# Part B of a gated two-branch kernel: Q, K and the attention output in five dense chunks of 128 rows, regrouped by head through DRAM

## The chip, the cores and the metric

The kernel runs on one core of one Trainium2 chip. The metric is the device time of one execution in microseconds (us). Every time of an instruction below comes from one profiled execution and is counted from the start of its span.

## The reference, cut to what matters

The output is `g * A(x) + (1 - g) * B(x)` for 2048 tokens of 640 features, with `g = sigmoid(sum(x * gate_w))`. A is a recurrent attention over 64 segments of 32 tokens. B is a local, dilated attention of 32 heads of 20 features, and it is the part that the change touches:

```python
H = 32; Dh = D // H                 # 640 / 32 = 20
W, dil = (8, 2)
qkv = (x @ wqkv).reshape(B, S, 3, H, Dh).transpose(2, 0, 3, 1, 4)
q, k, v = qkv[0], qkv[1], qkv[2]
...
idx = pos[:, None] - off[None, :]   # the 8 tokens at distance 0, 2, .., 14
logits = jnp.einsum('bhsd,bhswd->bhsw', q, kg) * Dh ** -0.5
logits = jnp.where(mask[None, None, :, :], logits, -1000000000.0)
attn = _softmax(logits, axis=-1)
o = jnp.einsum('bhsw,bhswd->bhsd', attn, vg)
return o.transpose(0, 2, 1, 3).reshape(B, S, D) @ wo
```

## The kernel before, in words

The program has three stages in a row: part B (`part_b`, lines 87 to 332), a prepass that multiplies the last rows of all segments by the weights of A (`prepass`, from L508), and the recurrent part A (`part_a`, from L611), which takes most of the time. The prepass needs all eight PSUM banks, so its first matmul (L531) waits for the last PSUM read of part B.

Part B walks over five blocks of tokens: four of 484 and one of 112 (`shape_of`, L202). In each block it walks over eight groups `g` of four heads. A head has 20 features, and four heads lie in the four 32-row quarters of a 128-partition tile; the 12 spare rows of each quarter are zeros. The weights of Q and K are spread to that form once (copies at L136, zeros at L131), and so are the rows of `wo` (zeros by GpSimd at L139, four loads of 20 partitions at L142). In step `(b, g)` of the loop at L310 these parts are called in this order:

- `make_xT` (L160) transposes the 512 tokens of the next x block by TensorE (L165), forms the gate (L176 to L183), and stores two rearranged copies for part A (L194, L199). At its middle it loads the next four x tiles from ScalarE's queue (L116).
- `make_v` (L209) forms V of the next block: 40 matmuls of 320 columns (L219), in a full block.
- `proj` (L226) forms Q and K of the next step: five matmuls each (L232), 484 columns for Q and 498 for K. Q is copied out by VectorE (`bqT`), K by ScalarE (`bkT`), both through the helper at L74/L76.
- `scores` (L240) forms the scores of four heads, 16 small matmuls (L250). ScalarE exponentiates them (L255, two instructions of 968 columns), and VectorE applies the band mask (L259).
- `values` (L262) works on the step before: 16 matmuls against a tile of ones give the softmax sums, 16 against V the outputs (L272). ScalarE forms the reciprocal by Ln and Exp (L277, L278), VectorE multiplies (L280) and writes the tile `OT`.
- `out_tile` (L283) multiplies 128 tokens of `OT` by `wo`: 16 matmuls of 320 columns (L290). One half is copied out by ScalarE (L295), the other by VectorE (L297), and ScalarE's queue stores the result (L299). There are 16 such tiles.

`proj`, `make_v`, `make_xT` and `out_tile` share two PSUM banks (`bank`, L108), so each waits for the copy-out of the last but one. The sums and the outputs have one bank each, the scores two pairs.

A scheduler orders the instructions of each engine at build time; it keeps roughly the order of the program but moves an instruction ahead where it is ready. Each engine then runs its own list strictly in order. That holds for transfers too: SyncE (SP) issues nearly all of them, and one that must wait holds up all transfers behind it; a transfer issued from ScalarE holds up ScalarE's arithmetic. `load_early` (L433) stands at the start of part B: it loads nine tiles of A's weights (L430, 4.2 MB) and makes copies of 21 further pieces from DRAM to DRAM (L441), from which part A later streams.

Of the kernel before, what the change touches and what calls it, by code (L numbers as in the profile page):

```python
# [10 lines left out]
BF = mybir.dt.bfloat16  # L11
# [16 lines left out]
class _K:  # L28
# [58 lines left out]
    def part_b(self):  # L87
# [11 lines left out]
        with ExitStack() as ctx:  # L99
# [25 lines left out]
            wop = wp.tile([128, 8, 640], BF, name="wo_pad")  # L125
            wqk = [wp.tile([128, KC, 32, 32], BF, name=f"w{n}_pad") for n in "qk"]
            xT = wp.tile([128, KC, HALO + S], BF, name="xT")
            OT = wp.tile([128, 8, S], BF, name="OT")
            wsrc = self.wqkv.rearrange("(c p) f -> p c f", p=128)
            for n, w in enumerate(wqk):  # L130
                nc.gpsimd.memset(w[:, :, :, 20:32], 0.0)  # L131
                raw = OT[:].rearrange("p g t -> p (g t)")[:, 3200 * n:3200 * n + 3200]
                (nc.scalar, nc.sync)[n].dma_start(raw.rearrange("p (c f) -> p c f", c=KC), wsrc[:, :, 640 * n:640 * n + 640])
                for kc in range(KC):
                    eng = (nc.vector, nc.gpsimd)[(KC * n + kc) % 2]
                    eng.tensor_copy(w[:, kc, :, 0:20], raw[:, 640 * kc:640 * kc + 640].rearrange("p (h d) -> p h d", d=20))  # L136
            nc.sync.dma_start(gw[:], self.gate_w.rearrange("(c p o) -> p c o", p=128, o=1))
            nc.scalar.dma_start(wv[:], wsrc[:, :, 1280:1920])
            nc.gpsimd.memset(wop[:], 0.0)  # L139
            wosrc = self.wo.rearrange("(g h d) f -> h d g f", h=4, d=20)  # L140
            for hh in range(4):
                nc.sync.dma_start(wop[32 * hh:32 * hh + 20, :, :], wosrc[hh])  # L142
# [81 lines left out]
            qk = {}  # L224

            def proj(b, g):  # L226
                nq, nu, c0 = shape_of(b)
                nt = nq * nu
                for n, (o0, nn) in enumerate(((c0 + HALO, nt), (c0, nt + HALO))):
                    ps = bank(F32, "ps_bqk")  # L230
                    for kc in range(KC):
                        nc.tensor.matmul(ps[:, 0:nn], lhsT=wqk[n][:, kc, 4 * g:4 * g + 4, :].rearrange("p h d -> p (h d)"),  # L232
                                         rhs=xT[:, kc, o0:o0 + nn], start=(kc == 0), stop=(kc == KC - 1))
                    t = wk.tile([128, BQ + HALO], BF, name="b" + "qk"[n] + "T", bufs=3)
                    self.evac(t[:, 0:nn], ps[:, 0:nn], "dve" if n == 0 else "act")
                    qk[b, g, n] = t
# [3 lines left out]
            def scores(b, g):  # L240
                nq, nu, c0 = shape_of(b)
                nk = nq + 7
                qT, kT = qk.pop((b, g, 0)), qk.pop((b, g, 1))
                for hp in range(2):
                    ps = psS.tile([128, 2, 512], F32, tag="S", name="ps_bS")
                    for u in range(nu):
                        a = 242 * (u // 2) + u % 2
                        for r in range(2):
                            rs = slice(64 * hp + 32 * r, 64 * hp + 32 * r + 32)
# [12 lines left out]
            def values(b, g):  # L262
# [4 lines left out]
                P = [Ps.pop((b, g, hp)) for hp in range(2)]  # L267
                for u in range(nu):
                    for out, z in ((pz, True), (po, False)):
                        for hh in range(4):  # L270
                            h = 4 * g + hh
                            nc.tensor.matmul(out[32 * hh:32 * hh + 32, nq * u:nq * u + nq],  # L272
                                             lhsT=ones[0:nk, :] if z else Vs[b, u][0:nk, 20 * h:20 * h + 32],
                                             rhs=P[hh // 2][0:nk, hh % 2, nq * u:nq * u + nq], start=(u == 0),
                                             stop=(u == nu - 1), tile_position=(0, 32 * hh), skip_group_check=True)
# [3 lines left out]
                dst = OT[:, g, BQ * b:BQ * b + nt].rearrange("p (l n q) -> p l q n", l=nu // 2, q=2)  # L279
                nc.vector.tensor_tensor(out=dst, in0=po[:, 0:nt].rearrange("p (l q n) -> p l q n", q=2, n=nq),  # L280
                                        in1=rz[:, 0:nt].rearrange("p (l q n) -> p l q n", q=2, n=nq), op=ALU.mult)

            def out_tile(ti):  # L283
# [3 lines left out]
                for f in range(2):  # L287
                    ps = bank(F32, "ps_bo")
                    for g in range(8):
                        nc.tensor.matmul(ps[:, 0:320], lhsT=OT[:, g, 128 * ti:128 * ti + 128],  # L290
                                         rhs=wop[:, g, 320 * f:320 * f + 320], start=(g == 0), stop=(g == 7))
# [13 lines left out]
            with tc.issue_after(self.first_store):  # L305
                self.load_early()
            make_v(0)
            proj(*steps[0])
            ti = 0
            for i, (b, g) in enumerate(steps):  # L310
                if g == 2 and b + 1 < S // 512:
                    make_xT(b + 1)
# [6 lines left out]
                if g == 6 and i + 8 < len(steps):  # L319
                    make_v(b + 1)  # L320
                if i + 1 < len(steps):
                    proj(*steps[i + 1])
# [3 lines left out]
                if g >= 1 and b > 0 and 128 * (ti + 1) <= BQ * b:  # L326
                    out_tile(ti)
                    ti += 1
# [104 lines left out]
    def load_early(self):  # L433

        for k in self.early:
            self.load(k, self.wres.tile([128, self.width(k)], BF, name="wres_" + "_".join(map(str, k)))[:])
        so = STREAM
        for i, k in enumerate(so):
            scr = self.dram.tile([128, self.width(k)], BF, name=f"wscr{i}")
            for d, src in self.sources(k, scr[:]):  # L440
                self.nc.sync.dma_start(d, src)  # L441
            self.wscr[k] = scr[:]
# [726 lines left out]
```

## Time and profile before

| | |
|---|---|
| time, median of 3 runs | 1613.4 us (1610.96 to 1613.96) |
| the profiled execution | 1609.81 us, of which its span is 1608.1 us |
| TensorE matmul busy | 1503.2 us (93%) |
| VectorE / ScalarE / GpSimd busy | 829.6 / 668.1 / 215.0 us |
| first exponential of part B (L255) | 31.79 us |
| first matmul of the prepass (L531) | 233.75 us |
| transfers issued from SP: L430 of `load_early` | 28.97 to 50.13 us |
| the copies from DRAM to DRAM (L441) | 50.17 to 80.83 us |

The table of stretches used below gives for each stretch its length, the busy time and number of instructions of each engine, the granted TensorE clock, the mean busy share of the 16 DMA engines and the GB/s that they moved. A line of the timeline gives start, duration, engine, line of the program, operation, output and input tiles, count, and in brackets how long the engine was idle before it and what it waited for. Records of neighbouring ScalarE instructions overlap by about 0.1 us, so the distance between two starts is what one costs.

### The profile page before, as it was taken

How to read it: one execution, taken by the hardware profiler on the slowest of the kernel's cores; microseconds unless marked ns; L12 is line 12 of the kernel's file. 1: busy time of each engine (PE TensorE's matmuls, PEld its weight loads, DVE VectorE, ACT ScalarE, POOL GpSimd, SP SyncE). 2: the span in 40 equal slices, each digit the busy share in tenths (PEclk: the TensorE clock that was granted, in tenths of full speed). 3: DMA queues.
4: the chain of work that ended last, by engine and by line, in shares of the span. 5: the costliest groups of instructions: out<-in, count | busy, mean ns of one | idle time of the engine just before them, and what ended most of it. 6: DMA issues, size and time to landing. Idle time of an engine off the chain costs nothing. (4 is left out here: it accounts for less than half of the span.)

```text
span 1608.1 us, 92193 instructions
## 1 busy us (share of the span) xinstructions
PE 1503.2 (93%) x37462; PEld 851.1 (53%) x37477; DVE 829.6 (52%) x2263; ACT 668.1 (42%) x1735; POOL 215.0 (13%) x403
## 2 busy tenths in 40 slices
PE   6988899978689999999999999999999999999979
PEld 3545554433345555555555555555555555555557
DVE  4646543322345655655655555555555655655520
ACT  3855752212234444444444444444444443444430
POOL 4002000001011111111111111111111111111100
PEclk9999999989899999999999999999999999999989
DMA  5941029989989999999999999999999999999980
GB/s 159 211 132 55 18 76 277 239 196 285 267 258 333 332 321 332 329 329 325 334 325 333 325 324 329 329 322 332 325 312 332 328 318 332 330 322 331 323 217 16
DMA packets 431326, 438.67 MB, mean 273 GB/s; under 512 B 184720, under 2 KB 298408, under 8 KB 431256
## 3 DMA queue, kind: packets, MB, share of 16 engines
q1 hardware_dynamic: 326968, 389.78, 74.2%
q10 hardware_dynamic: 93024, 31.07, 8.1%
q0 software_dynamic: 11264, 16.83, 3.5%
q8 instruction: 51, 0.84, 0.2%
q14 instruction: 19, 0.16, 0.0%
HBM read 403.79 MB, written 38.86 MB: 275 GB/s over the span
## 5 line engine op out<-in xcount | busy, mean ns | idle before, releaser
L736 ACT CAST aP<-psx 128x512 bf16<-128x512 f32 x128 | 68.8, 589 | 357.6 <-PE psx L729 334.6
L891 PEld LDWEIGHTS <-aP 128*32 128x32 bf16 x6144 | 164.2, 97 | 64.5 <-ACT aP L870 18.0
L827 PE MATMUL psm<-wlate_v,aHa 128*32 128x512 bf16 x2048 | 185.8, 380 | 0.4 <-issue 0.4
L729 PEld LDWEIGHTS <-aHa 128*32 128x32 bf16 x4608 | 115.9, 96 | 120.8 <-PE psm L729 20.7
L891 PE MATMUL psm<-wlate_oa,aP 128*32 128x384 bf16 x2560 | 168.7, 331 | 0.0
L751 DVE STREAM_TRANSPOSE aK<-aP 128x512 bf16<-128x512 bf16 (+1 forms) x256 | 135.1, 547 | 7.2 <-ACT aP L736 0.6
L891 PE MATMUL psm<-wst,aP 128*32 128x384 bf16 (+1 forms) x896 | 122.0, 307 | 9.5 <-DMA wst<-wscr 9.5
L891 PE MATMUL psm<-wlate_ob,aP 128*32 128x256 bf16 x2688 | 126.2, 274 | 0.5 <-issue 0.5
L729 PE MATMUL psx<-wlate_k,aHa 128*32 128x512 bf16 x1152 | 120.1, 380 | 0.0
L748 DVE STREAM_TRANSPOSE aP<-aP 128x512 bf16<-128x512 bf16 (+1 forms) x128 | 74.1, 579 | 85.8 <-ACT aP L736 85.8
L827 PE MATMUL psm<-wlate_v,aHb 128*32 128x512 bf16 x1152 | 115.7, 380 | 0.0
L870 DVE CAST aP<-psx 128x128 bf16<-128x128 f32 (+2 forms) x192 | 75.5, 421 | 77.2 <-PE psx L858 77.0
L729 PEld LDWEIGHTS <-aHb 128*32 128x32 bf16 x3072 | 73.3, 96 | 63.3 <-issue 2.1
L836 ACT CAST aP<-psm 128x256 bf16<-128x256 f32 (+1 forms) x192 | 85.9, 447 | 50.3 <-PE psS L781 47.4
L870 ACT CAST aP<-psS 128x384 bf16<-128x384 f32 (+2 forms) x192 | 65.3, 375 | 67.9 <-PE psx L858 52.6
L667 POOL DMA_DIRECT2D aVz<-zpk_dram x64 | 35.6, 556 | 426.5 <-PE psm L729 218.4
L729 PE MATMUL psx<-wst,aHa 128*32 128x512 bf16 x512 | 87.9, 381 | 0.4 <-DMA wst<-wscr 0.3
L729 PE MATMUL psx<-wlate_k,aHb 128*32 128x512 bf16 x768 | 78.4, 384 | 0.0
L852 PEld LDWEIGHTS <-aP 32*128 32x128 bf16 (+1 forms) x4096 | 44.1, 97 | 64.8 <-DVE aK L818 31.2
L660 POOL DMA_DIRECT2D aK<-xh_dram x63 | 34.9, 554 | 316.5 <-PE psm L827 281.1
L76 DVE CAST ZS<-ps_pre 128x512 bf16<-128x512 f32 x48 | 33.0, 692 | 82.6 <-PE ps_pre L531 76.8
L827 PE MATMUL psm<-wst,aHb 128*32 128x512 bf16 x384 | 74.2, 380 | 1.5 <-issue 1.5
(187 smaller groups left out, 3469.9 us busy)
## 6 DMA issues: line engine op xcount, KB each, us to landing
wst<-wscr SPq DMA_DIRECT2D x965, 256.0 KB, 4.6
wst<-wscr SPq DMA_DIRECT2D x384, 192.0 KB, 3.9
aP<-zpk_dram SPq DMA_DIRECT2D x64, 192.0 KB, 4.1
zpk_dram<-ZS ACTq DMA_DIRECT2D x5, 2048.0 KB
aVz<-zpk_dram POOLq DMA_DIRECT2D x64, 96.0 KB, 4.3
wlate_k<-in_A_Wk_dram SPq DMA_DIRECT2D x8, 512.0 KB
wres_q<-in_A_Wq_dram SPq DMA_DIRECT2D x7, 512.0 KB
wst<-in_A_Wk_dram SPq DMA_DIRECT2D x14, 256.0 KB
```

Of the source, the lines that this page charges most:

```text
L76: nc.vector.tensor_copy(out, in_)
L660: nc.gpsimd.dma_start(xh, row(self.xh_dram, s))
L667: nc.gpsimd.dma_start(vz[:], row(self.zpk_dram, s)[:, 768:1152])
L729: burst([nc.tensor.matmul(pq[32 * j:32 * j + 32, :], lhsT=hT[kc], rhs=sl[j], start=(kc == 0), stop=(kc == KC - 1), tile_position=(0, 32 * ...
L736: nc.scalar.copy(st[i], pqs[i])
L748: nc.vector.transpose(P[p][:, 1:5, c0:c1, :].rearrange("p b c i -> p c b i"), x)
L751: nc.vector.transpose(KT[:, c0:c1, :].rearrange("p c k -> p (c k)"), x)
L827: burst([nc.tensor.matmul(pvs[t][32 * j:32 * j + 32, :], lhsT=hT[kc], rhs=sl[j], start=(kc == 0), stop=(kc == KC - 1), tile_position=(0, 3 ...
L836: (nc.vector.tensor_copy if t == 0 else nc.scalar.copy)(Px[t][:, cs], pvs[t][:, cs])
L852: ms.append(nc.tensor.matmul(out[:, r, t, :], lhsT=v_block(2 * h + r, t)[ks, f0 - 128 * t:f1 - 128 * t], rhs=E[ks, par, EA.start + 40 * r: ...
L870: (nc.scalar.copy, nc.vector.tensor_copy)[g](x.rearrange("p (j c q) -> p j c q", j=2, q=32), pairs[g][:, :, 0:240].rearrange("p j (c q) -> ...
L891: ms.append(nc.tensor.matmul(pso[part][32 * jj:32 * jj + 32, 0:n], lhsT=oT_slot(R // 2, j, 3 * (R % 2) + t), rhs=self.o_weights(osl, part, ...
```

## The change

The weights of Q, K and `wo` are no longer spread to quarters of 32. Q, K and the output are computed in five dense chunks of 128 rows, and put into or taken out of the by-head form by transfers through DRAM. So that these transfers have time, Q and K are formed one block ahead (five chunks in the steps `g` = 0 to 4), and output tiles are formed later. The first block's Q and K, and a second `make_xT`, come ahead of the loop. `load_early` is queued behind the first block's round trip, and the copies from DRAM to DRAM leave it: eight, eight and five of them follow the round trips of later blocks. The softmax sums take one matmul per head over all columns. The core of the diff (left out are the plain loads of the dense weights, and the split of the copies into a function of their own):

```diff
-            wop = wp.tile([128, 8, 640], BF, name="wo_pad")
-            wqk = [wp.tile([128, KC, 32, 32], BF, name=f"w{n}_pad") for n in "qk"]
+            woc = wp.tile([128, KC, 640], BF, name="wo_sb")
+            wqk = [wp.tile([128, KC, 640], BF, name=f"w{n}_sb") for n in "qk"]
...
-            OT = wp.tile([128, 8, S], BF, name="OT")
+            OTc = wp.tile([128, KC, S], BF, name="OTc")
+            OTb = [wp.tile([128, 8, BQ], BF, name=f"OT{i}") for i in range(2)]
+            QK = [[[wp.tile([128, 4, BQ + HALO], BF, name=f"b{n}T{i}{h}") for h in range(2)] for i in range(2)] for n in "qk"]
...
-            nc.gpsimd.memset(wop[:], 0.0)
...
+            def heads(t, half, hh):
+
+                return t[320 * half:320 * half + 320].rearrange("(g h d) t -> h d g t", g=4, h=4)[hh]
...
+            def proj(b, n, c):
...
+                ps = bank(F32, "ps_bqk")
+                for kc in range(KC):
+                    nc.tensor.matmul(ps[:, 0:nn], lhsT=wqk[n][:, kc, 128 * c:128 * c + 128], rhs=xT[:, kc, o0:o0 + nn],
+                                     start=(kc == 0), stop=(kc == KC - 1))
+                t = wk.tile([128, BQ + HALO], BF, name="b" + "qk"[n] + "c", bufs=3)
+                self.evac(t[:, 0:nn], ps[:, 0:nn], "dve" if n == 0 else "act")
+                nc.sync.dma_start(qk_dram[b, n][128 * c:128 * c + 128], t[:, 0:nn])
+                if c in (2, 4):
+                    half = c // 4
+                    for hh in range(4):
+                        self.last_qk = nc.sync.dma_start(QK[n][b % 2][half][32 * hh:32 * hh + 20, :, 0:nn],
+                                                         heads(qk_dram[b, n], half, hh)).ins
...
+                for hh in range(4):
+                    nc.tensor.matmul(pz[32 * hh:32 * hh + 32, 0:nt], lhsT=ones[0:nk, :], rhs=P[hh // 2][0:nk, hh % 2, 0:nt],
+                                     start=True, stop=True, tile_position=(0, 32 * hh), skip_group_check=True)
...
+                if g % 4 == 3:
...
+                    for hh in range(4):
+                        nc.sync.dma_start(heads(ot_dram[b], half, hh),
+                                          OTb[b % 2][32 * hh:32 * hh + 20, 4 * half:4 * half + 4, 0:nt])
+                    cs = slice(2 * half, 2 + 3 * half)
+                    nc.sync.dma_start(OTc[:, cs, BQ * b:BQ * b + nt],
+                                      ot_dram[b][:].rearrange("(c p) t -> p c t", p=128)[:, cs])
...
-                    for g in range(8):
-                        nc.tensor.matmul(ps[:, 0:320], lhsT=OT[:, g, 128 * ti:128 * ti + 128],
-                                         rhs=wop[:, g, 320 * f:320 * f + 320], start=(g == 0), stop=(g == 7))
+                    for c in range(KC):
+                        nc.tensor.matmul(ps[:, 0:320], lhsT=OTc[:, c, 128 * ti:128 * ti + 128],
+                                         rhs=woc[:, c, 320 * f:320 * f + 320], start=(c == 0), stop=(c == KC - 1))
...
             make_xT(0)
-            with tc.issue_after(self.first_store):
+            for c in range(KC):
+                for n in range(2):
+                    proj(0, n, c)
+            with tc.issue_after(self.last_qk):
                 self.load_early()
+            make_xT(1)
             make_v(0)
-            proj(*steps[0])
...
-                if g == 2 and b + 1 < S // 512:
-                    make_xT(b + 1)
...
-                if g == 6 and i + 8 < len(steps):
-                    make_v(b + 1)
-                if i + 1 < len(steps):
-                    proj(*steps[i + 1])
+                if g == 6:
+                    if b + 2 < S // 512:
+                        make_xT(b + 2)
+                    if b + 1 < nb:
+                        make_v(b + 1)
+                if g < KC and b + 1 < nb:
+                    proj(b + 1, 0, g)
+                    proj(b + 1, 1, g)
+                    if g == KC - 1:
+                        with tc.issue_after(self.last_qk):
+                            for k in copies[:8]:
+                                self.copy_scratch(k)
+                            del copies[:8]
                 scores(b, g)
                 if i > 0:
                     values(*steps[i - 1])
-                if g >= 1 and b > 0 and 128 * (ti + 1) <= BQ * b:
+                if (b + 2 < nb and g >= 3 or b + 2 == nb and g in (5, 7) or b + 1 == nb and g in (2, 5)) and \
+                        128 * (ti + 1) <= BQ * min(b, nb - 2):
                     out_tile(ti)
                     ti += 1
```

By these conditions, three output tiles fall into block 1, four into block 2, two each into blocks 3 and 4, and five come behind the loop.

## The prediction

> **What bounds the kernel now.** The page names TensorE (1503 us busy of 1608), but that is an average over stages. I asked for stretches: the five blocks of part B, cut at the first exponential of each block. Part B ends where the prepass's first matmul starts, at 233.75, and nothing of A overlaps it on TensorE. So what part B gains, the kernel gains.
>
> ```profile
> core 0: us, PE busy (x) PEld busy (x) DVE busy (x) ACT busy (x) POOL busy (x), PEclk, DMA share, GB/s
> 31.79:68.64 36.85, 34.11 (x516) 18.67 (x514) 23.18 (x41) 28.36 (x47) 3.11 (x3) 1.00 0.85 191
> 68.64:118.79 50.15, 43.71 (x596) 24.75 (x592) 25.66 (x48) 31.61 (x53) 3.54 (x7) 0.93 0.55 149
> 118.79:169.19 50.40, 45.16 (x612) 26.09 (x608) 32.56 (x51) 31.43 (x52) 8.94 (x8) 0.97 0.16 45
> 169.19:209.76 40.57, 35.93 (x547) 21.48 (x543) 23.11 (x43) 28.27 (x47) 0.21 (x2) 0.98 0.10 31
> 209.76:233.75 23.99, 23.14 (x351) 15.17 (x350) 11.83 (x40) 13.39 (x46) 0.00 (x0) 0.88 0.09 30
> ```
>
> TensorE looks like the bound here too. Three single steps, from exponential to exponential, say otherwise: one with an output tile, a plain one, and one whose next projection is small.
>
> ```profile
> 92.26:98.42 6.16, 5.42 (x90) 3.15 (x82) 3.21 (x6) 3.81 (x7) 0.00 (x0) 1.00 1.01 282
> 98.42:101.74 3.32, 3.11 (x62) 1.48 (x50) 2.17 (x5) 3.29 (x6) 0.00 (x0) 1.00 0.05 16
> 204.04:206.90 2.86, 2.31 (x74) 1.68 (x60) 1.52 (x3) 2.86 (x6) 0.00 (x0) 1.00 0.12 44
> ```
>
> In the last two ScalarE has no gap (3.29 of 3.32, 2.86 of 2.86): these steps are ScalarE's, not TensorE's. The timeline shows why the first is long.
>
> ```profile
> 92.26 1.85 ACT L255 ACTIVATE bP<-ps_bS 128x968 bf16<-128x968 f32 x2
> ...
> 92.59 2.35 PE L290 MATMUL ps_bo<-wo_pad,OT 128*128 128x320 bf16 x16
> ...
> 95.12 0.51 ACT L295 ACTIVATE bo<-ps_bo,omg_sb 128x320 bf16<-128x320 f32 x1
> ...
> 95.69 1.18 PE L232 MATMUL ps_bqk<-xT,wq_pad 128*128 128x484 bf16 x5 [0.74 <-ACT bo L295]
> ...
> 96.70 1.21 PE L232 MATMUL ps_bqk<-xT,wk_pad 128*128 128x498 bf16 x5
> ...
> 97.95 0.57 ACT L74 CAST bkT<-ps_bqk 128x498 bf16<-128x498 f32 x1 [2.32 <-PE ps_bqk L232]
> ```
>
> It is a ring: ScalarE reaches the tile's copy-out only after its exponentials, the next projection waits for that bank, and ScalarE then waits 2.32 for K. The 16 output matmuls are no part of the ring.
>
> **The change, part by part.** The sum is made against the profiled execution: 1609.8 us, of it 1608.1 span and 1.7 around it. The median shown is 3.6 above that.
>
> *Matmuls removed.* Per full block 30 of 80 projections go, and 6 of 16 matmuls per output tile. At 1.01 us per five (95.69 to 96.70) and 2.35 per 16 that is 4 x 6.1 + 16 x 0.88 = 38 us of TensorE time. By the steps above most of it hides under ScalarE. The sums' 16 matmuls of 121 columns become four of 484: as many columns, nothing gained, and Ln waits for ScalarE anyway.
>
> *Start, 31.8 now.* Twelve projections instead of four precede the first scores: +8 x 1.03 = 8.2. A second `make_xT` comes ahead: +4.0, from steps (0,1) and (0,2), which take 6.32 and 4.27 around one instead of 3.32 each. The GpSimd memset of `wo_pad` goes; beside it (16.43 to 20.79) a VectorE addition on 4 columns (L180) took 4.54 instead of 0.17 and held V's copy-outs: -4.4. Weights come dense, so ten spreading copies go too; `wo`'s 0.8 MB now competes with x, about 3 us at 250 GB/s, and I let the two cancel. First exponential: 39.6. The round trip is hidden if Q and K of half 0 are there by then: six chunks from about 15 (two at half clock) end at 23.5. A 162 KB store lands 2.2 to 3.1 us after issue (135.76 to 137.93, 96.46 to 99.54), four loads issue in 1.5, landing again 3: about 33. If the cover failed, each us late would cost one.
>
> *Block 0, 36.85 now.* One `make_xT` and one `make_v` as before; three steps lose K's copy-out, 3.32 to 2.86: 35.5.
>
> *Block 1, 50.15 now.* Three plain steps at 3.45 (they take 3.32 to 3.72), one ring of 6.16 at `g` = 3; the tiles at 4 and 5 have no projection behind them, so 2.86 + 0.51 + a wait of 0.6 for VectorE's half: 4.0 each. `make_xT` 4.0, `make_v` 6.3 (9.63 against 3.32), two steps of 2.86: 40.5. Part of the gain is the stall of step (1,2), below.
>
> *Block 2, 50.40 now.* 10.35 + 6.16 + 3 x 4.0 + 6.3 + 2.86, and the stall that a GpSimd copy of the prepass puts on VectorE (L520, 143.56; VectorE's L285 took 4.28), which no part of the change removes: 41.8.
>
> *Block 3, 40.57 now.* Its projections are for the 112-row block: five steps at 3.0, two tiles at 4.0, V 3.5, one step 2.86: 29.4. Here all four steps with tiles were rings of 6.16.
>
> *Block 4 and tail, 23.99 now.* Six small steps at 1.3 (0.99 and 1.69 today), two with a tile at 2.6, the last values 1.0. Then the last output goes to DRAM and back: 2 x 2.2 to 3.1 plus five issues at 0.4, so 6.4 to 8.2; four tiles that need only block 3 run beside it at some 1.75 each (1.4 matmul, rest the copy-outs): 7.2 in all. Then one tile, 2.3: 23.5.
>
> Sum: 39.6 + 35.5 + 40.5 + 41.8 + 29.4 + 23.5 = 210.3 against 233.75, **-23.4**. Three costs are to be added, which the trace of before shows only in part.
>
> *SP's queue.* A full block issues 36 transfers (10 stores, 16 loads, 8 and 2 for the output) at 0.36 to 0.40, 13 to 14 us, and stops six times for a landing, 13 to 19 us: it fits under 35 to 42. The copies sit in the same queue: the ten of Q and K took 50.17 to 68.83, so the first eight hold it 15 us; the outputs behind them are read 25 us later at (1,3). Worse placed is `load_early`: its 4.2 MB, 17 us at 249 GB/s, go right ahead of block 1's first stores. Q's chunk buffers are three; the fourth copy-out, on VectorE at about 50, waits for the first store, which lands at about 58 to 60. Bounds: 0, if the build-time order lets scores overtake, and 9. The timeline around 76 shows transposes and scores interleaved, so the order is movable: I take +3.
>
> *ScalarE's queue.*
>
> ```profile
> 79.09 4.35 ACTq L116 DMA_DIRECT2D x_sb<-in_A_x_dram  x3
> ...
> 83.48 0.17 ACT L179 ACTIVATE gz_sb<-ps_g 128x4 f32<-128x4 f32 x1 [4.11 <-DMA x_sb<-in_A_x_dram]
> ```
>
> Three x loads issued while the copies ran held ScalarE 4.1 us. In the new order the last x loads follow the first eight copies again: +4. Bounds 0 (the copies are through) and 4.1 for every such issue (rival below).
>
> *Clock.* The granted clock is 0.88 in the last stretch: after two steps with small projections it fell to half, and the matmuls at 212 run at 0.45 for 0.30. Now three steps of every block have no projection. At half clock one output tile took 3.95 (85.73) instead of 2.35; I charge that 1.6 once in each full block: +6. Bounds: 0, and 5.8 (a whole `make_v` doubled) per block.
> By the Trainium skill, "TensorE: Matmul & The Clock Gate", "Why this matters for your kernels", the clock drops only after TensorE idles for some 3 us. No gap in these steps is that long, so by that rule this term is 0 and the sum -16; the row at 212 speaks against it, since TensorE was never idle so long there.
>
> Total -23.4 + 3 + 4 + 6 = **-10.4**: 1599.4 on the profiled execution's scale, **1603.0** on that of the median.
>
> **The rivals.** A measurement here can tell about 0.2% (3.2 us) from no change.
>
> 1. *Forecast*, 1603.0, chance 0.38.
> 2. *The clock stays full* (the page's rule): 1613.4 - 16.4 = 1597. For it: the plain steps of block 0 ran at 1.00 throughout. Against: 0.88 in the last stretch. 0.20.
> 3. *TensorE is the bound after all*, and all 38 us go: 1575. For: its busy share in the blocks. Against: the ScalarE rows of the single steps. 0.08.
> 4. *`load_early` really blocks*: 9 instead of 3, and 3 more where the outputs wait behind the copies: -1.4, 1612, no change that can be told. 0.12.
> 5. *Slower: the two queues couple.* An out-tile store is issued in ScalarE's stream. If it must wait for SP's chain of round trips as the x loads waited for the copies, each costs 4.1 us of the engine that is the bound. Eleven tiles lie inside the loop. Three such waits eat the forecast; five give -10.4 + 20.5 = +10, 1623.5. For: the 4.11 above. Against: the out-tile stores of blocks 2 and 3 went out among few other transfers and never waited so for one; how they fare among 36, the trace can't show. 0.22.
>
> That the change doesn't do what it says is no rival here: every matmul and transfer counted is in the code.
>
> **How the numbers follow.** Faster: forecast, 2 and 3, 0.66. Same: 0.12. Slower: 0.22. The range runs from 1585, which takes in rival 2 with all three costs near their lower ends but not rival 3, to 1624, the price of rival 5.
>
> **What would show it.** Right: first exponential at 39 to 41; the step without projection or tile at 2.86; blocks 1 and 3 shorter by about ten each; the prepass starting near 223, and its own 115 us to the V part unchanged. `load_early`: a wait of VectorE's Q copy-out for a store near 50. Rival 2: clock 1.00 in blocks 0 to 3. Rival 3: plain steps shorter than ScalarE's 2.86. Rival 5: ScalarE idle for a DMA at L299 in blocks 1 and 2. Wrong altogether: scores that wait for their Q and K loads at a block's start, or a prepass that starts earlier but loses it again for lack of weights.

## The result and the profile after

The changed kernel takes 1626.9 us (1624.9 to 1631.4, five runs) against 1613.4 us before (1608.3 to 1614.0, five runs): a ratio of 1.0098, 95% interval 1.0074 to 1.0123. It is slower by one per cent, and the forecast, its sign and its range missed it.

The same view as before, five stretches from one block's first exponential to the next (to 0.1 us); the columns are length, busy time and count of TensorE's matmuls and weight loads, VectorE, ScalarE, GpSimd, then granted clock, DMA share and GB/s:

```profile
core 0: us, PE busy (x) PEld busy (x) DVE busy (x) ACT busy (x) POOL busy (x), PEclk, DMA share, GB/s
38.86:86.70 47.84, 38.34 (x426) 20.25 (x425) 22.57 (x38) 29.51 (x46) 3.54 (x7) 0.75 0.66 178
86.70:125.10 38.40, 31.26 (x373) 16.38 (x372) 21.30 (x36) 27.46 (x42) 0.43 (x4) 0.78 0.78 168
125.10:179.40 54.30, 45.87 (x496) 26.16 (x496) 27.46 (x50) 30.98 (x51) 3.77 (x5) 0.84 0.58 147
179.40:213.40 34.00, 28.44 (x364) 16.44 (x359) 18.89 (x34) 25.04 (x42) 0.00 (x0) 0.70 0.37 89
213.40:247.50 34.10, 21.96 (x226) 12.13 (x224) 14.22 (x38) 12.18 (x39) 4.72 (x1) 0.79 0.60 177
```

The prepass starts at 247.5 instead of 233.8. These 13.7 us are about the difference of the medians (13.5). The profiled execution was the slowest of the five, 21.6 us above the profiled one of before; of the other 8 us, 1.4 lie in the prepass (116.8 us to its first V matmul, 115.4 before) and 6 in the recurrent part, which the change does not touch. Against before, the start takes 7.1 us more, block 0 11.0 more, block 1 11.8 less, block 2 3.9 more, block 3 6.6 less, and the last stretch 10.1 more.

The start is now 38.9 instead of 31.8, as forecast (39.6). But fewer matmuls (2067 instead of 2729 in part B) keep TensorE busy for 193.6 us, hardly less than the 199.9 before, with the clock at half for 95 us of the stretch from 25 to 250 us, where it was for 17.

The single steps are about as short as forecast (3.45 with projections, 2.86 without): one with projections, one plain, one plain of which a part is at half clock.

```profile
89.29:92.87 3.58, 3.40 (x50) 1.67 (x47) 2.60 (x5) 3.40 (x6) 0.00 (x0) 1.00 1.15 165
96.07:98.23 2.16, 1.33 (x29) 0.67 (x30) 1.44 (x3) 2.12 (x3) 0.00 (x0) 1.00 0.75 109
98.23:101.42 3.19, 2.16 (x43) 1.28 (x45) 1.99 (x4) 3.19 (x6) 0.00 (x0) 0.84 1.04 210
```

What is long is the last step of each block: 23.7, 18.1, 23.8 and 14.9 us from the first exponential of (b,7) to that of (b+1,0), where it was 3.7, 3.7, 3.7 and 2.9 before. The timeline of TensorE shows what fills the first of them:

```profile
66.74 0.60 PE L279 MATMUL ps_bO<-bP,bV 128*32 128x121 bf16 x16 [0.56 <-DVE OT L287]
68.76 2.17 PE L232 MATMUL ps_bqk<-xT,wq_sb 128*128 128x484 bf16 x5 [1.42 <-DVE bqc L76]
...
72.80 0.53 PE L159 MATMUL ps_xT<-ident,x_sb 128*128 128x128 bf16 x4
...
76.93 7.16 PE L213 MATMUL ps_bv<-wv_sb,xT 128*128 128x320 bf16 x40
83.99 1.18 PE L232 MATMUL ps_bqk<-xT,wq_sb 128*128 128x484 bf16 x5
...
86.16 0.43 PE L255 MATMUL ps_bS<-bqT,bkT 20*128 20x121 bf16 x16
```

After the last values of the block come, one behind the other, the fifth chunk's projections (68.76), the transposes (72.80), V (76.93) and the next block's first chunk (83.99), and only then scores again. In the kernel before each of these stood between two steps' scores. Now TensorE's list, fixed at build time, has the scores of `g` = 4 to 7 ahead of them. All of them need the two shared PSUM banks, and a bank is free only when the chunk in it is copied out, for which one of three chunk buffers must be stored (e1 below bears this out for block 0). The timeline of SP's queue shows why a store comes late:

```profile
40.36 12.45 SPq L462 DMA_DIRECT2D wres_q<-in_A_Wq_dram  x9
...
53.57 1.42 SPq L236 DMA_DIRECT2D bq_dram<-bqc  x1
```

The output meets the same queue one block later: the last heads of block 0 are multiplied on VectorE at 67.46, and their stores are issued behind eight copies.

```profile
94.89 2.50 SPq L475 DMA_DIRECT2D wscr<-in_A_Wk_dram  x1
...
103.76 2.23 SPq L294 DMA_DIRECT2D ot_dram<-OT  x4
...
110.25 0.37 SPq L297 DMA_DIRECT2D OTc<-ot_dram  x1
```

From 38 us to the prepass SP issued 66 transfers in 57 us of issuing before, and issues 228 in 123 us now (summed from the trace's SP rows).

### The profile page after: what moved, and what is told of

Its sections match the earlier page's. It is cut to its first block, busy times and chain, and to the rows that moved or that the text cites. A ratio compares the mean times of both kernels' runs of the same rounds, so it can differ in the third digit from the quotient of the medians.

```text
span 1629.6 us, 91195 instructions
## 1 busy us (share of the span) xinstructions
PE 1502.7 (92%) x36815; PEld 839.0 (51%) x36815; DVE 813.5 (50%) x2243; ACT 664.1 (41%) x1720; POOL 203.5 (12%) x395
## 5 line engine op out<-in xcount | busy, mean ns | idle before, releaser
L861 PE MATMUL psm<-wlate_v,aHa 128*32 128x512 bf16 x2048 | 189.5, 380 | 0.3 <-issue 0.3
L763 PEld LDWEIGHTS <-aHa 128*32 128x32 bf16 x4608 | 116.0, 96 | 117.9 <-issue 18.2
L861 PEld LDWEIGHTS <-aHa 128*32 128x32 bf16 x2304 | 54.5, 96 | 46.6 <-issue 16.2
```

Source lines behind the costliest of these rows:

```text
L763: burst([nc.tensor.matmul(pq[32 * j:32 * j + 32, :], lhsT=hT[kc], rhs=sl[j], start=(kc == 0), stop=(kc == KC - 1), tile_position=(0, 32 * ...
L861: burst([nc.tensor.matmul(pvs[t][32 * j:32 * j + 32, :], lhsT=hT[kc], rhs=sl[j], start=(kc == 0), stop=(kc == KC - 1), tile_position=(0, 3 ...
```

## The experiments

Two measures are given for each. The ratio to the kernel before, timed on the same chip, is the verdict. The **start of the prepass** (its first matmul) in the profiled execution says what part B took; it leaves out the recurrent part, which took from 1195 to 1209 us behind the prepass's last matmul in these profiles without any edit to it. But it is one execution of each kernel, and it scatters too: the changed kernel, e9 and e18, which are written the same up to there, have their first exponential at 38.9, 39.2 and 38.1. Differences of 2 to 3 us are therefore not read as effects.

| kernel | ratio (95%) | prepass starts |
|---|---|---|
| before | 1 | 233.8 |
| changed | 1.0098 (1.0074 to 1.0123) | 247.5 |
| e1 six buffers | 1.0042 (1.0023 to 1.0062) | 241.7 |
| e2 order | 1.0055 (1.0038 to 1.0072) | 238.3 |
| e3 six buffers, order | 1.0028 (1.0013 to 1.0043) | 239.6 |
| e4 sums alone | 1.0013 (0.9999 to 1.0028) | 231.0 |
| e5 output half alone | 0.9957 (0.9932 to 0.9982) | 227.4 |
| e6 Q and K half alone | 1.0110 (1.0081 to 1.0140) | 249.3 |
| e7 e3 with order both ways, bulk one per step | 1.0018 (1.0000 to 1.0036) | 243.2 |
| e8 e7, output from GpSimd | 1.0064 (1.0036 to 1.0092) | 247.9 |
| e9 changed, filler | 1.0067 (1.0050 to 1.0084) | 247.6 |
| e10 e7, filler | 1.0040 (1.0019 to 1.0062) | 246.5 |
| e11 e5, copies handed out | 0.9909 (0.9888 to 0.9931) | 220.7 |
| e12 before, less projection work | 0.9773 (0.9756 to 0.9790) | 201.6 |
| e13 e7's order, copies behind part B | 1.0202 (1.0165 to 1.0239) | 227.5 |
| e14 e13, Q/K loads from GpSimd | 1.0131 (1.0093 to 1.0170) | 225.1 |
| e15 e13, V and tiles spread | 1.0213 (1.0176 to 1.0251) | 231.4 |
| e16 before, copies handed out | 0.9950 (0.9928 to 0.9971) | 231.3 |
| e17 e7's order, four copies at a time | 1.0041 (1.0016 to 1.0067) | 241.0 |
| e18 changed, copies behind part B | 1.0310 (1.0260 to 1.0361) | 239.4 |

### Order and buffers: e1, e2, e3

e1 gives the chunks six buffers. e2 leaves three, and puts each step's scores behind that step's projections, V or tile in TensorE's list; e3 does both.

```diff
-                t = wk.tile([128, BQ + HALO], BF, name="b" + "qk"[n] + "c", bufs=3)
+                t = wk.tile([128, BQ + HALO], BF, name="b" + "qk"[n] + "c", bufs=6)
...
-                scores(b, g)
+                with tc.issue_after(self.pe):      # e2, e3: last matmul of proj, make_v or out_tile
+                    scores(b, g)
```

> The changed kernel with six chunk buffers per Q and K instead of three, nothing else. Theory A (TensorE's instructions are laid out so that projections, transposes, V and output tiles of a block pile up behind its last scores, because the fourth chunk's copy-out waits for a store that sits in SP's queue behind load_early): in block 0 the projections no longer wait for a buffer, the step behind scores (0,7), 23.7 us in the changed kernel, falls to under 8, and block 0 goes from 47.8 to some 36 to 39; blocks 1 and 2 keep their long last steps, since those wait for the output round trip. 1626.9 - 9 = 1618 us. Theory B (the loss is TensorE's half clock in the light steps): the same clock, under 4 us gained, 1623 to 1627. Theory C (the scores wait for the Q and K round trip at each block's start): buffers change nothing there, 1625 to 1628. Theory D (ScalarE held by its own transfers, the rival on record): no change, 1627.

> The changed kernel, three buffers as there, but with each step's scores put behind that step's projections, V and the output tile of the step before in TensorE's order, so that TensorE's list runs step by step and nothing piles up behind scores (b,7). No wait and no transfer is taken away. Theory A: the long last steps (23.7, 18.1 and 12.6, 23.8, 14.9 us) dissolve into the steps; block 0 still meets the store behind load_early, now at scores (0,4), so it gains least; blocks 1 to 3 lose some 8 to 12 us each, against which stand tiles that now really wait for the output round trip. 1627 - 17 = 1610 us. Theory B: the steps hold more work for TensorE, so the clock stays up, and the gain is the same in kind: the granted clock of part B then tells how much, 0 gain if the clock stays as it is. Theory C: longer, as scores that were ahead now wait as well, 1630. Theory D: no change, 1627.

> Both edits: six chunk buffers, and TensorE's list step by step. Theory A: this is the order for which the prediction's sum was made, so the prepass starts at some 223 to 230 (233.75 before, 247.5 in the changed kernel): 1603 to 1610 us. Theory C: still 1620 or more, with TensorE waiting for Q or K loads in the first step of each block. Theory D: ScalarE's waits for transfers stay, 1620 or more.

e1 went the way of theory A in block 0: the step behind (0,7) falls from 23.7 to 10.9 us (under 8 was expected), block 0 to 40.0. The last steps of blocks 1 and 2 stay at 21.3 us each, so there something else than the buffers makes the pile; what, these runs don't show. Part B is 5.8 us shorter. e2 gained more in part B (9.2 us, where theory A had 17): the long last steps are gone (3.3 to 3.6 us), yet blocks 0 and 1 take 48.7 and 47.7 us, no less than in the changed kernel. Its list holds TensorE where the store is late, and the wait that the prediction had named "near 50" is there to see, on TensorE and on VectorE:

```profile
60.16 2.17 PE L232 MATMUL ps_bqk<-xT,wq_sb 128*128 128x484 bf16 x5 [8.38 <-DVE bqc L76]
```

```profile
59.45 0.66 DVE L76 CAST bqc<-ps_bqk 128x484 bf16<-128x484 f32 x1 [6.85 <-DMA bq_dram<-bqc]
```

Theories C and D gave no gain for these, and are out as the main cause. But e3 did not reach theory A's 1603 to 1610 (223 to 230): order and buffers are 7.9 of at least 13.7 us. What e3's TensorE still waited for was the output:

```profile
PE ps_bo L309 <- DMA OTc<-ot_dram: 20.1, 4, 7.2
```

### The halves of the change: e4, e5, e6

e4 puts the new sums into the kernel before. e5 adds the output half to it; Q and K stay as they were. e6 is the changed kernel with the output left in SBUF in the padded form. The diffs are the parts of the change itself.

> The kernel before with one part of the change alone: the softmax sums by one matmul of 484 columns per head instead of four of 121. The prediction's step (as many columns, Ln waits for ScalarE anyway): within 2 us of the kernel before, 1611 to 1615. If TensorE is what bounds the steps (rival 3 on record), 36 x 12 matmuls fewer at some 0.03 us of issue each: 1605 or less.

> The kernel before with the output half of the change alone (and the one-matmul sums): heads go to DRAM and back, five output matmuls of 128 rows per half tile, output tiles placed as in the changed kernel; Q and K as before, with 32 rows per head and two buffers ahead. Here the copies lie in SP's queue long before the output and TensorE's list stays step by step. Theory A (pile-up and queueing behind SP's bulk transfers): little is lost; the tail pays the last round trip, 4 to 6 us, the rings of blocks 1 and 2 give 2 to 4 back: 1609 to 1617 us against some 1612. If the output round trip by itself is what costs (TensorE waits for it wherever it lies), tiles wait in every block: 1620 or more.

> The changed kernel with the output half undone: the output stays in SBUF with 32 rows per head, eight output matmuls per half tile, no output transfers; Q and K in five chunks through DRAM as in the change, three chunk buffers. Theory A: the pile-up behind (0,7) stays, as it comes from the chunk buffers and load_early; tiles 0 and 3 no longer wait for transfers, so blocks 1 and 2 lose less, and the tail is short: 1612 to 1619 us. If the loss lay in the output round trip alone: 1600 to 1606. If it lay in Q and K alone: 1625 or more.

The sums alone make no difference that can be told, as predicted (the prepass's start, 2.8 us earlier, lies within its scatter). The output half makes the kernel **faster**, by more than expected (6.4 us in part B). The Q and K half carries the whole loss, and more of it than any reading expected but the last. Of e6's 15.6 us, 10.3 lie before the first exponential (42.1 against 31.8): e6 pays for the early projections and also keeps the zeros and the four loads of the padded `wo`, which the whole change drops.

### SP's queue: e7, e8, e13, e14, e17, e18

In these runs, e18 apart, there are six buffers, and the list goes step by step both ways: projections, V, transposes and tiles also stand behind the scores of the step before. e7 hands out the early loads and the copies one per step, e17 the copies four at a time behind each return of the output, e13 puts all the copies behind part B. e8 issues the output's transfers from GpSimd, e14 Q's and K's loads. e18 moves the copies in the changed kernel and does nothing else. Where an expectation speaks of 24 copies, the kernels make 21, in 26 transfers.

```diff
-                        with tc.issue_after(self.last_qk):
-                            for k in copies[:8]:
-                                self.copy_scratch(k)
-                            del copies[:8]
...
+            with tc.issue_after(self.back):        # e13, e18: the last return of the output
+                for k in copies:
+                    self.copy_scratch(k)
```

> The changed kernel with six chunk buffers, TensorE's list step by step on both sides (scores behind that step's projections, projections, V, transposes and tiles behind the scores of the step before), and SP's bulk transfers (9 early weight loads and 24 copies) handed out one per step behind that step's other transfers instead of nine at once and eight at once. Theory A: no wait of 7 to 10 us for a store or for the output is left; block 0 at 36 to 39, blocks 1 and 2 at 38 to 43, prepass at 225 to 231: 1602 to 1608 us where the kernel before has some 1612. If SP's queue is full in any order (36 transfers with their stops plus eight copies of 1.5 us are 40 to 45 us per block): blocks of 42 to 47 us, no long single wait but many of 2 to 4, 1613 to 1618.

> As the run before, and the output round trip issued from GpSimd's queue instead of SP's (ten transfers per block). Theory A: SP's queue loses some 8 us per block; where the run before still had tiles waiting for the output, they no longer do: 0 to 5 us better than that. If SP's queue was not the limit there: the same within 2 us; if GpSimd's descriptor work delays its own copies of xh and zx: worse by a few us.

> The changed kernel with six chunk buffers, TensorE's list step by step, and all 24 copies moved behind the last output transfer of part B, so that SP's queue carries only the round trips, the early loads and the stores of x in part B. What counts is the start of the prepass (233.8 before, 247.5 in the changed kernel, 239.6 with buffers and order, 243.2 with one bulk transfer per step); the copies then lie beside the prepass and may hold its weights, which is read apart. Theory E (SP's one queue, in which each transfer waits for the data of the one ahead, is what delays the output and the chunks): prepass at 226 to 232. If what is left lies on TensorE (transposes and V of a block in one step behind the scores, 15 to 18 us where they are spread over the steps in the kernel before): 238 to 242, as with the copies.

> As the run before, and the 16 loads of Q and K per block are issued from GpSimd's queue, the stores of the chunks and the output round trip stay on SP. Theory E: SP loses 6 us and four waits per block, output and chunks go out without waiting for each other: 3 to 8 us earlier than the run before. If GpSimd's own price per transfer takes it back, or the round trips had cover: the same within 2 us, or some us later with scores waiting at a block's start.

> The whole change with six chunk buffers, TensorE's list step by step, and the copies four at a time behind each return of the output. Theory E: between the run without copies in part B (prepass at 227.5) and the one with eight at once (239.6): 231 to 238, 1609 to 1616, so the whole change at its best here is no faster than before. If the place alone counts, and not how much SP issues: 227 to 230, 1603 to 1608.

> The changed kernel with only the copies moved behind part B: three chunk buffers and TensorE's list as it was. Theory A (order and buffers cost by themselves): the step behind (0,7) keeps its 23 us, as load_early still lies ahead of the first store; blocks 1 and 2 lose the wait for the output but keep the pile: prepass at 238 to 243, against 227.5 with order and buffers. Theory E alone (only the copies cost): 227 to 231. The prepass itself is held by the copies, as in the earlier run.

e7 and e17 fell on the side of "full in any order": 243.2 and 241.0, no better than eight at once (239.6), and e17 missed what theory E gave for it. In e7 one long wait for the output is left all the same (10.0 us). e8 was worse than e7 on both measures, although TensorE's waits for the output fell from 14.9 to 4.1 us; what took that back was not found. e13 was the run that decided: with the copies out of the queue, part B ends at 227.5, inside theory E's 226 to 232, with SP issuing 199 transfers in 92 us. TensorE's waits for the output fell to

```profile
PE ps_bo L309 <- DMA OTc<-ot_dram: 8.3, 2, 4.4
```

The kernel as a whole is slower all the same: beside the copies the prepass takes 151.0 us to its first V matmul instead of 115.4, and TensorE waits 40.0 us in it for weights:

```profile
PE ps_pre L568 <- DMA wst<-in_A_Wq_dram: 23.2, 1, 23.2
PE ps_pre L568 <- DMA wst<-in_A_Wk_dram: 9.1, 1, 9.1
PE ps_pre L568 <- DMA wlate_q<-in_A_Wq_dram: 7.7, 1, 7.7
```

e14 took 2.4 us more off, less than theory E gave and within the scatter. e18 separates the causes, as theory A expected it (238 to 243) and theory E alone did not. Together, with the start of the prepass:

| | copies in part B | copies behind it |
|---|---|---|
| list and buffers as changed | 247.5 | 239.4 |
| six buffers, step by step | 239.6 to 243.2 | 227.5 |

The three runs of the lower left cell (e3, e17, e7) differ in the order and in how the copies are handed out; e17 and e13 differ in the place of the copies alone, e18 and e13 in buffers and order alone. Mending the list gives 4 to 9 us (e2 the most), moving the copies alone 8, both 20. So the order of TensorE's list and the copies in SP's queue both cost, and together they seem to cost more than one by one (3 to 8 us, the lower end near the scatter).

Whether the copies delay the rest by SP's time to issue them or also by the DMA engines' time was not separated. There is a third way, which none of the theories names. In the changed kernel SP's transfers wait for out-tile stores that ScalarE issued, other work altogether:

```profile
SPq L294 <- DMA bsc_dram<-bo: 6.1, 1, 6.1
SPq L475 <- DMA bsc_dram<-bo: 4.9, 1, 4.9
SPq L236 <- DMA bsc_dram<-bo: 4.9, 2, 2.7
SPq L240 <- DMA bsc_dram<-bo: 4.7, 2, 2.7
```

In the trace the transfers of both queues take the same eight completion semaphores (the counters that tell of a landing) in turn, and these waits are on them. So the two queues are coupled: six waits, 20.6 us by the profile's account, of which the two of L240 (4.7 us) may be for their own data as well. e13 has such waits too. What they cost was not tested.

### The clock: e9, e10

Both write the 16 values matmuls three times into the same bank in steps with little work, where they change no number.

```diff
-                for u in range(nu):
+                for _ in range(3 if g >= 4 or b >= 3 else 1):
+                    for u in range(nu):
```

> The changed kernel, and the 16 values matmuls are written three times over into the same bank for heads of g = 4 to 7 and of block 3 on: the same numbers, only more work for TensorE, in the time in which it would wait for Ln and Exp. Theory B' (the granted clock follows how busy TensorE was: in ten traces, of 427 windows of 3.41 us at full clock that were 0.8 busy or more, two were followed by half clock, of 37 under 0.45 busy, 35 were): busier steps keep the clock, V, transposes and projections at the blocks' ends run at full clock, mean clock of part B up from some 0.80 towards 0.9, 1627 - 8 = 1619 us or less. Theory A (order and queues alone): added work can only cost, up to 32 x 0.8 us, or nothing where it is hidden: 1627 to 1635.

> The kernel with spread bulk transfers, six buffers and TensorE's list step by step (1616.9 where the kernel before had 1611.0), and values written three times over as in the run before. Theory B': what that kernel still lost (V of block 1 at half clock, 9.1 us between 61.1 and 70.2, the output tile of block 3, the tail) falls by some 10 us: 1604 to 1609. Theory A: what is left there is waiting for the output, which added matmuls don't shorten: 1616 to 1622.

The counts of windows in the first of these texts are off; the last section has them, counted over all kernels. The filler did raise the clock (71 us at half instead of 95 in e9, 61 instead of 85 in e10) and moved the start of the prepass by +0.1 and +3.3 us. e9's shorter time as a whole (the interval overlaps the changed kernel's) does not come from part B. e10 came out where theory A put it (1620.8 us). And e13 runs below full clock in four of its five stretches (0.83, 0.89, 1.00, 0.81, 0.73), with 55 us at half, and is 20 us shorter than the changed kernel. Theory B' is not borne out: no time could be bought back by raising the clock with filler. But the filler takes time itself, and in e13 half clock fell along with the waits, so what half clock costs by itself stays open.

### TensorE's own work: e12, e15

```diff
-                    for kc in range(KC):
+                    for kc in range(1):            # e12, in the projections of the kernel before
```

> The kernel before with only the first of the five contraction chunks in each Q and K projection: four fifths of the sum over the features are left out, so some 57 us of TensorE's matmul time go from part B, and no transfer, wait or order changes. The prediction's step (ScalarE is the bound, TensorE's time hides under it): 5 to 15 us faster, 1598 to 1608. Rival 3 on record (TensorE the bound): 40 us faster or more, 1570. Theory B' (less work lets the clock fall to half, which gives the time back): part B with the clock at half in the greater part of it, and 1608 to 1620, no gain or a loss.

> As the first run of these, and TensorE's work of a block is spread: transposes in step 5, V in two halves in steps 6 and 7, output tiles of blocks 1 and 2 in steps 5 to 7 instead of 3 to 6. If the pile of transposes and V in one step costs (the second reading of the first run): its 15 to 18 us in block 0 fall to 8 to 10, blocks 1 and 2 lose their waits for the output: prepass 6 to 12 us earlier than the first run. Theory E alone: tiles in later steps wait less for the output, 2 to 5 us earlier.

e12 is the run that speaks most directly against the prediction's reading of the single steps. The table of stretches from the first instruction to the prepass, of the kernel before and of e12:

```profile
0.00:233.75 233.75, 199.91 (x2729) 116.46 (x2730) 130.55 (x244) 139.02 (x249) 32.02 (x47) 0.96 0.40 104
```

```profile
0.00:201.60 201.60, 165.50 (x2409) 95.66 (x2410) 128.04 (x244) 135.67 (x249) 33.27 (x47) 0.92 0.47 121
```

The projections are busy for 52.5 us less (80.9 to 28.4). TensorE as a whole is busy for 34.4 us less, as other matmuls take longer, with the clock at half for 34 us instead of 17 (from 25 to 250 us). Part B is 32.2 us shorter, with ScalarE and VectorE nearly unchanged. In the kernel before, then, some three fifths of the time taken from TensorE count; it is not so that most of it hides under ScalarE. The whole gains 37.7 us, near to rival 3's 40. e15 asked whether V and the transposes in one step were what remained in e13; part B got longer (231.4), which neither forecast had, and that reading is not borne out.

### The version that beats both: e11, and its control e16

e11 is e5 with the copies four at a time behind each return of the output; e16 is the kernel before with its copies eight at a time behind stores of x.

```diff
+                    with tc.issue_after(back.ins):
+                        for k in self.copies[:4]:
+                            self.copy_scratch(k)
+                        del self.copies[:4]
```

> The kernel with the output half alone (1605.4 where the kernel before had 1611.0), and its 24 copies handed out in SP's queue four at a time behind each return of the output instead of all behind the early loads. Theory A: the stalls that the copies make in block 1 there (x loads and the gate held 4.9 us on ScalarE, projections at 81 and 93 waiting) go, block 1 falls from 53 to 42 to 46 us: 1596 to 1601 us. If those stalls come from the output's own transfers: 1604 to 1607.

> A control: the kernel before, unchanged but that its 24 copies are handed out in SP's queue eight at a time behind the second, third and fourth store of x instead of all behind the early loads. It tells what the handing out is worth without the change. Theory E (bulk transfers in SP's queue cost where something waits in that queue): nothing of before's scores or tiles waits for SP, only x loads and the gate on ScalarE, 4 to 7 us in block 1: prepass from 233.8 to 227 to 231, 1605 to 1610 where the kernel before has 1612. Then the output half keeps some 6 us as its own gain in the fastest version so far (prepass at 220.7). If handing out is worth as much as there: 220 to 224.

e11 takes 1598.3 us, 0.9909 of the kernel before, as expected. How much of that is handing out alone? By the start of the prepass in e16, 2.4 us of the 13.1, no more than the scatter; by the timed runs, 0.9950, some 8 of e11's 15 us. The two measures disagree, so the output half's own share in e11 stays open; alone, in e5, it gave 0.9957. The stretches of e11's blocks 1 and 3, cut at the first scores, columns as above (before, cut at the first exponentials: 50.15 and 40.57):

```profile
64.30:108.90 44.60, 39.64 (x479) 21.49 (x478) 25.62 (x48) 31.39 (x51) 3.48 (x7) 1.00 0.56 121
...
160.30:192.00 31.70, 29.26 (x403) 15.11 (x404) 21.24 (x37) 27.02 (x43) 0.17 (x2) 1.00 0.20 52
```

## Why the prediction was wrong, point by point

**The step that failed** is "SP's queue", with its "+3" and its sentence "it fits under 35 to 42", and the block sums that rest on it. It reckoned SP's issuing for one block and let the copies and the round trips share the queue at no cost beyond `load_early`. Measured, the order (with the buffers) and the copies cost 20 us of part B together (247.5 against 227.5): the 36 transfers, the copies and the stops don't fit, and what waits there holds banks, so that TensorE's work piles up behind (b,7), shown for block 0 by e1 and argued for the others. The clause "if the build-time order lets scores overtake" was read the wrong way round. Scores did overtake, and that did not hide the wait but moved the projections, V and tiles to where nothing runs beside them. The queue is not all of it: even in e13 the prepass starts 17 us behind the 210.3 to which the blocks add up before the three costs.

*Matmuls removed.* "Most of it hides under ScalarE" was wrong: e12 gives 32.2 us for 52.5 us of projections. Three single steps were read as the rule; that the steps with V, transposes and tiles, which make up the rest of a block, are TensorE's is argued from that, not measured step by step. Rival 3 was nearer to what bounds the kernel before, and the change still lost, because the gain was given back to the order, the copies, the start and the tail.

*Start*: right, 38.9 for 39.6. It is a price of the Q and K half: the first exponential comes at 37.7 to 38.7 in e1 to e3 and e13, and at 29.0 in e11.

*Block 0*: 47.8 for 35.5, the pile. *Block 1*: 38.4 for 40.5, near by luck, as its tiles, transposes and V partly lie in block 2. *Block 2*: 54.3 for 41.8, the pile again. *Block 3*: 34.0 for 29.4; the same tiles without Q and K in chunks take 31.7 (e11), which fits the reading of the rings as ScalarE's and VectorE's copy-outs but does not test it.

*Block 4 and tail*: 34.1 for 23.5. In the changed kernel TensorE is idle for 12.1 us of it (0.9 before), but hardly for a return of the output (its weight loads wait 1.1 us); a wait of 4.4 us for one is in e13, where the stretch takes 31.9. Two gaps of TensorE, 2.30 us at 223.74 and 3.90 before the prepass, end with VectorE or ScalarE waiting for an out-tile store: all tiles go through two `bo` buffers, five tiles stand behind the loop, and the store issued at 239.73, for which the last tile waits, lands 7 us later, beside the weight loads that SP issues from 236 on.

```profile
246.78 0.53 ACT L314 ACTIVATE bo<-ps_bo,omg_sb 128x320 bf16<-128x320 f32 x1 [6.08 <-DMA bsc_dram<-bo]
...
247.49 0.61 PE L565 MATMUL ps_pre<-zT,wres_q 128*128 128x512 bf16 x1 [3.90 <-DVE bo L316]
```

*`load_early`*: the wait was named and is there (8.38 us on TensorE in e2), nearer the upper bound of 9 than the 3 taken. *Outputs behind the copies*, 3 us in rival 4: moving the copies gave 8 us, and 12 to 16 with the list mended.

*ScalarE's queue*, +4: ScalarE waited four times for a transfer, 3.3 and 1.4 us in the blocks, 2.7 and 6.1 in the tail, all at copy-outs of out tiles or of the K chunk beside one. That is rival 5's row, and in the tail, as shown, it costs; in the blocks the waits are fewer and shorter than the three of 4.1 that rival 5 needed, and that its 1623.5 is near the measured 1626.9 is luck. Up to the tail it is not the cause: from 38 to 226 us e6 shows no such wait and starts the prepass latest of all, and e13 shows five, 14.9 us in all, and is 20 us shorter in part B.

*Clock*, +6: half clock for 95 us, 17 before, far more than the term assumed; yet raising it moved the prepass by nothing (e9), so the size of the term stays open. The Trainium skill, "TensorE: Matmul & The Clock Gate", "Why this matters for your kernels", advises no idle gaps above some 3 us, as one idle window brings half clock; the traces here show drops without such a gap (last section).

*The rivals.* The clock stayed anything but full (2). 4 had the mechanism and a price too small. 5 had the two queues coupled, which the trace shows, but put its price on ScalarE. None had the copies and the list together, which is why the range ended at 1624.

## What to carry to other kernels

A queue that one engine issues in order is a resource like an engine: add up its issuing and its stops over the whole stretch, with every bulk transfer that shares it, before costing a round trip at nothing. A wait there shows up elsewhere, as work on another engine that was moved behind it at build time and now stands alone; look at the order of that engine's list and not only at waits, of which such a pile shows few. To learn whether an engine's time counts, take work from that engine alone in the kernel before: one such run says more than reading three steps.

## What the runs showed of the hardware

**The granted clock follows how busy TensorE was, not only whether it was idle.** The trace's records of it change in steps of 3.41 us. Counted over the twenty traces of this case from 25 to 260 us: of 766 such windows at full clock in which TensorE was at least 0.8 busy, 761 were followed by full clock; of 222 between 0.45 and 0.8, 143; of 42 below 0.45, 2. At half clock, none of 134 windows below 0.8 was followed by full clock, and 98 of 109 that were at least 0.97 busy were. Of 121 drops up to 250 us, 117 had no gap of 3 us between matmuls in the two windows before. So in these traces a light stretch without such a gap can lose the clock, and it mostly takes a nearly full window to get it back.

**Large DRAM-to-DRAM copies are dear for the queue that issues them**: the changed kernel's first eight, of 256 KB, held SP's queue from 84.19 to 97.44, 1.66 us each, against a median of 0.38 for the store of a chunk. Its 16 copies of V's and the output's weights, of 64 to 192 KB, took 0.61 at the median.
